# Reordering the seven products of a channel-mixing matmul, with one more PSUM bank, and making the next batch's activations one slot sooner

## The chip, the cores and the metric

The kernel runs on one core of a Trainium2 chip. The metric is the device time of one execution in microseconds (us). A profiled execution also has a span, from its first to its last traced instruction; the device time is 1.8 to 2.1 us longer than the span. In the program, TensorE writes into PSUM tiles (the text calls one of them a bank); the tiles that the other engines make lie in SBUF.

## The reference, cut to what matters

Eight batches of a linear attention feed an MLP mixer. Only the last line matters here.

```python
x = attention(q, k, v)                       # 8 batches x 576 positions x 512
u = x + (relu(x.T @ w_tok1) @ w_tok2).T      # token mixing
out = u + relu(u @ w_ch1) @ w_ch2            # channel mixing, 512 -> 1536 -> 512
```

Inputs and output are float32; the kernel multiplies in bfloat16.

## The kernel before

TensorE is the engine to keep busy. While it does the channel mixing of one batch, the other engines prepare the next batch. The second matmul of the channel mixing, h1 @ w_ch2, is cut into 2 x 2 quadrants and done with seven products instead of eight (in the manner of Strassen and Winograd): fewer matmuls, but sums of quadrants for VectorE, GpSimd and ScalarE. `a11`..`a22` are the quadrants of h1, `quad(i, j)` those of the weights, `t1`, `t2`, `t3`, `t4` sums of these made once, `s1` and `s2` sums of the a's made for every batch, in two parts each. One product is 12 matmuls, 1.31 us. `channel7` does this for six batches and, with `fine=True`, for the tail: the last 64 positions of every batch together, whose 1 MB of output ends the program.

```python
def channel7(uT, u, store, by_slot, hooks, fine=False):
    ...                                       # step(): runs what hangs on the next slot
    for mi in range(NCH):                     # 12 hidden blocks, L667
        c_ps = psM.tile([P, 512], F32, name="c_ps", tag="psM")
        ...
        relu(by_slot[mi], h1[:, mi, :], c_ps)
        if mi == NCH - 2:                     # first part of both sums
            s_part(s1, nc.vector.tensor_add, a21, a22, 0)
            s_part(s2, nc.vector.tensor_sub, s1, a11, 0)
        if mi == NCH - 1:                     # second part of both sums, L652
            s_part(s1, nc.vector.tensor_add, a21, a22, 1)
            s_part(s2, nc.vector.tensor_sub, s1, a11, 1)
        step()
    Dk = bank()                               # then seven products, L657
    ...                                       # fine: A in two halves
    A = bank()
    product(A, a11, quad(0, 0), True)         # first product
    nc.scalar.copy(va, A)
    nc.vector.tensor_sub(a21, a11, a21)
    step()
    product(Dk, a22, t4, True)                # second
    nc.scalar.copy(vb, Dk)
    nc.gpsimd.tensor_sub(u22, u22, vb)
    step()
    Bk = bank()
    product(Bk, s2, t2, True)                 # third: the first reader of s2
    nc.vector.tensor_add(va, Bk, va)
    nc.vector.tensor_sub(s2, a12, s2)
    step()
    C = bank()
    product(C, s1, t1, True)                  # fourth: the first reader of s1
    ...
```

Between two batches the work of the next one (`n`) hangs on these slots. `u_all(i)` is three steps: VectorE adds the token mixing to x (L466), GpSimd casts it to bfloat16 (L265), and the SP queue issues a transposing DMA into `uT` (L473), which the next batch's hidden blocks (L667) read.

```python
at(10, n.u_all, 0)
at(11, n.u_all, 1)                            # slot 11: behind the second part of s1 and s2
...
def store_tail(j, u, n=1, cs=slice(0, Dm)):   # each call: one store on the SP queue, one on ScalarE's
    for c, eng in ((0, nc.sync), (1, nc.scalar)):
        eng.dma_start(out=rows[:, 2 * j + c:2 * (j + n):2, cs], in_=u[c::2, j:j + n, cs])
```

Of the kernel before, what the change touches and what calls it, by code (L numbers as in the profile page):

```python
# [9 lines left out]
F32 = mybir.dt.float32  # L10
# [7 lines left out]
PLAN = """  # L18
feat.0.k.4.2.0.D feat.0.q.0.2.0.A feat.0.q.2.2.1.A feat.0.q.3.2.1.A feat.0.q.4.2.1.D feat.0.q.3.2.0.A
feat.0.q.2.2.0.A mkid ld.1.q.2 warm.0.tr.1.1.43 turn.0.1.1 feat.0.k.3.2.0.A feat.0.k.4.2.1.D turn.0.1.0  # L20
feat.0.q.1.2.1.D feat.0.q.4.2.0.A feat.0.q.1.2.0.A feat.0.k.2.2.0.D feat.0.k.1.2.1.D cast.0.0.3.0.P
warm.0.tr.2.1.7 turn.0.2.1 turno.0.2.1.A feat.0.k.0.2.1.D cast.0.3.2.0.D feat.0.k.1.2.0.D turno.0.1.0.A
feat.0.q.0.2.1.D warm.0.tr.0.0.45 turn.0.0.0 feat.0.k.0.2.0.D turn.0.2.0 turno.0.2.0.D feat.0.k.3.2.1.A
feat.0.k.2.2.1.A cast.0.0.3.1.A turn.0.0.1 wt1 turno.0.1.1.D wt2 cast.0.3.2.1.P kvm.0.1 kvo.0.1.D turno.0.0.1.A
turno.0.0.0.A kvm.0.0 kvo.0.0.A num.0.0.1 numo.0.0.1 feat.1.q.1.2.1.A num.0.2.1 numo.0.2.1 num.0.0.0 numo.0.0.0
# [34 lines left out]
def kernel(  # L60
# [11 lines left out]
    nc = tc.nc  # L72

    B, H, S, D = q.shape
    Dm = H * D
    _, D_tok = moe_w_tok1.shape
    _, D_ch = moe_w_ch1.shape
    P = 128
# [33 lines left out]
    psA = ctx.enter_context(tc.tile_pool(name="psA", bufs=2, space=bass.MemoryType.PSUM))  # L112
# [19 lines left out]
    def heads(g):  # L132
        return slice(0, H) if g == 2 else slice(g * HH, (g + 1) * HH)
# [23 lines left out]
    for n, (t, g) in enumerate(LOADS0):  # L157
        d = load(0, t, heads(g), nc.gpsimd if FIRST == "P" else nc.sync)
# [108 lines left out]
    def relu(eng, dst, src):  # L267
        if eng == "A":
            nc.scalar.activation(dst, src, AF.Relu)  # L269
        else:  # L270
            nc.vector.tensor_relu(dst, src)  # L271
# [342 lines left out]
    K2, D2 = NCH // 2, Dm // 2  # L614
    t2, t3, t4 = (const.tile([P, K2, D2], BF16, name=f"t{i}") for i in (2, 3, 4))

    def quad(a, b):
        return wc2[:, a * K2:(a + 1) * K2, b * D2:(b + 1) * D2]

    t1 = quad(0, 1)  # L620
# [7 lines left out]
    def channel7(uT, u, store, by_slot, hooks, fine=False):  # L628
        h1 = one.tile([P, NCH, 4 * P], BF16, name="h1")
        slot = 0  # L630

        def step():
            nonlocal slot
            for f in hooks.get(slot, ()):
                f()
            slot += 1

        def tok(a, b):
            return h1[:, a * K2:(a + 1) * K2, b * 2 * P:(b + 1) * 2 * P]

        a11, a12, a21, a22 = tok(0, 0), tok(1, 0), tok(0, 1), tok(1, 1)
        s1 = one.tile([P, K2, 2 * P], BF16, name="s1")
        s2 = one.tile([P, K2, 2 * P], BF16, name="s2")
        va = w2r.rearrange("p n s -> p (n s)").bitcast(F32)[:, :2 * D2].rearrange("p (a b) -> p a b", a=2)
        vb = one.tile([P, 2, D2], F32, name="vb")
        vc = one.tile([P, 2, D2], F32, name="vc")
        u11, u12 = u[:, 0:2, :D2], u[:, 0:2, D2:]
        u21, u22 = u[:, 2:4, :D2], u[:, 2:4, D2:]

        def s_part(dst, f, a, b, n):  # L650
            ks = (slice(0, 4), slice(4, K2))[n]
            f(dst[:, ks], a[:, ks], b[:, ks])  # L652

        def product(ps, a, b, first, jjs=(0, 1)):
            for jj in jjs:
                for ki in range(K2):
                    nc.tensor.matmul(ps[jj] if isinstance(ps, list) else ps[:, jj], a[:, ki, jj * P:(jj + 1) * P], b[:, ki],  # L657
                                     start=(first and ki == 0 and (jj == 0 or isinstance(ps, list))), stop=ki == K2 - 1,
                                     skip_group_check=True)

        def bank():
            return psM.tile([P, 2, D2], F32, name="m_ps", tag="psM")

        for mi in range(NCH):
            c_ps = psM.tile([P, 512], F32, name="c_ps", tag="psM")
            for ki in range(NCC):
                nc.tensor.matmul(c_ps, wc1[:, ki, mi * P:(mi + 1) * P], uT[:, :, ki, :],  # L667
                                 start=(ki == 0), stop=(ki == NCC - 1))
            relu(by_slot[mi], h1[:, mi, :], c_ps)
            if mi == NCH - 2:  # L670
                s_part(s1, nc.vector.tensor_add, a21, a22, 0)
                s_part(s2, nc.vector.tensor_sub, s1, a11, 0)
            if mi == NCH - 1:
                s_part(s1, nc.vector.tensor_add, a21, a22, 1)
                s_part(s2, nc.vector.tensor_sub, s1, a11, 1)
            step()
        Dk = bank()
        if fine:
            A = [bank()[:, 0], psA.tile([P, D2], F32, name="m2_ps", tag="psA")]
            for jj in range(2):  # L680
                product(A, a11, quad(0, 0), True, (jj,))
                nc.scalar.copy(va[:, jj], A[jj])
        else:
            A = bank()
            product(A, a11, quad(0, 0), True)
            nc.scalar.copy(va, A)
        nc.vector.tensor_sub(a21, a11, a21)
        step()
        product(Dk, a22, t4, True)
        nc.scalar.copy(vb, Dk)  # L690
        nc.gpsimd.tensor_sub(u22, u22, vb)
        step()
        Bk = bank()
        product(Bk, s2, t2, True)
        nc.vector.tensor_add(va, Bk, va)
        nc.vector.tensor_sub(s2, a12, s2)
        step()
        C = bank()
        product(C, s1, t1, True)
        nc.scalar.copy(vc, C)  # L700
        nc.vector.tensor_add(u12, u12, va)
        nc.gpsimd.tensor_add(u22, u22, vc)
        step()
        product(Dk, a21, t3, False)
        nc.vector.tensor_add(vb, Dk, va)
        step()
        wide = bass.AP(tensor=vb.tensor, offset=vb.offset, ap=[vb.ap[0], [D2, 2], [0, 2], [1, D2]])
        u2 = u[:, 2:4, :].rearrange("p j (a d) -> p j a d", a=2)
        product(C, s2, quad(1, 1), False)
        if fine:  # L710
            nc.vector.tensor_add(u2, u2, wide)
            store(2, u, 2)
            nc.vector.tensor_add(u12, C, u12)
            store(0, u, 2, slice(D2, Dm))
            step()
            for jj in range(2):
                product(A, a12, quad(1, 0), False, (jj,))
                nc.vector.tensor_add(u11[:, jj], A[jj], u11[:, jj])
            store(0, u, 2, slice(0, D2))
        else:  # L720
            nc.vector.tensor_add(u12, C, u12)
            step()
            product(A, a12, quad(1, 0), False)
            nc.vector.tensor_add(u11, A, u11)
            store(0, u, 2)
            nc.vector.tensor_add(u2, u2, wide)
            store(2, u, 2)
        step()
        step()

    def out_rows(b, par, j, n):
# [21 lines left out]
    for word in PLAN.split():  # L753
        name, *a = word.split(".")
        a = [int(x) if x.isdigit() else x for x in a]
# [37 lines left out]
    def hooks7(n, m, nxt, quads):  # L793
        h = {}

        def at(slot, f, *a):
            h.setdefault(slot, []).append(lambda: f(*a))
        if nxt is not None:
            at(0, load, nxt, "k")
            at(0, load, nxt, "q")  # L800
            at(16 if nxt == 5 else 9, load, nxt, "v")
        if n is not None:
            at(0, n.kv_all)
            for j in range(JA):
                at(2 + j, n.num_all, j)
            for j in range(JA):
                at(7 + j // 3, n.mix, j, 2)
            at(8, n.mix_out)
            at(10, n.u_all, 0)
            at(11, n.u_all, 1)  # L810
            at(18, n.u_all, 2)
        if m is not None:
            for j in range(JA):
                at(3 + j, m.cast, j, 1, 2, "P")
            for i, slot in enumerate((1, 2, 3, 4, 5, 6, 9, 10, 11, 12)):
                at(slot, m.feat, "q", i // 2, 2, i % 2, "A")
            for i, slot in enumerate((7, 7, 8, 8, 13, 14, 15, 16, 17, 17)):
                at(slot, m.feat, "k", i // 2, 2, i % 2, "D" if i < 4 else "A")
            at(12, m.turnx, 0, 2)
            at(14, m.turnx, 2, 2)  # L820
            at(15, m.turnx, 4, 1)
        if quads:
            for f, slot in zip(quad_weights(), (0, 0, 0, 8)):
                at(slot, f)
        return h
# [4 lines left out]
    for p in range(2, B):  # L830
        s = bt[p]
        n = bt[p + 1] if p + 1 < B else None
# [8 lines left out]
    _ = tile, bass_utils  # L841
# [30 lines left out]
```

## Time and profile before

| | before |
|---|---|
| time, median of 4 runs | 270.46 us (270.08 to 271.02) |
| span of the profiled execution | 267.7 us |
| TensorE busy | 254.9 us (95%) |
| first of the seven products starts, first `channel7` batch | 104.8 us |
| TensorE ends | 261.7 us |
| last store lands | 266.0 us |

The lines themselves are in the prediction. The table is read as three stretches: up to 105 us nothing in question happens; from there to TensorE's end lie six batches and the tail; after TensorE's end come the last sums and stores. The second and third stretches are what the change can touch.

### The profile page before, as it was taken

What the parts mean: (1) busy time and instruction counts of PE and PEld (TensorE: products, weight loads), DVE (VectorE), ACT (ScalarE), POOL (GpSimd) and SP (SyncE); (2) the same over time, 40 slices, a digit from 0 to 9 for tenths busy, and PEclk for the clock granted to TensorE, in tenths of its full rate; (3) what the DMA queues carried; (4) which work ended last, traced back from release to release, by engine and by line L of the source; (5) the groups of instructions that cost most, each with busy time, mean ns of one, the idle gap of its engine ahead of it and who ended that gap; (6) DMA issues with size and microseconds to landing.
All of it is one profiled execution on the core that took longest, in us unless ns stands there. A gap on an engine that the chain in (4) does not pass through costs nothing.

```text
span 267.7 us, 5480 instructions
## 1 busy us (share of the span) xinstructions
PE 254.9 (95%) x2165; PEld 161.5 (60%) x2181; DVE 202.3 (76%) x367; ACT 143.8 (54%) x236; POOL 76.7 (29%) x82
## 2 busy tenths in 40 slices
PE   6998999999999999999998999999999999999991
PEld 2785556456444555855585558645865585585580
DVE  6489798799892879969895869686958596564572
ACT  2796272473591576829782788378753423323410
POOL 2173070040033261702475007420710072030030
PEclk9999999999999999999999999999999999999997
DMA  6999999999999999999999995950393044003004
GB/s 201 361 255 165 243 258 229 365 224 214 343 287 181 288 374 369 128 182 326 288 326 183 306 366 131 178 196 2 74 204 156 0 81 162 14 2 157 0 2 158
DMA packets 79146, 53.41 MB, mean 200 GB/s; under 512 B 47761, under 2 KB 76689, under 8 KB 79121
## 3 DMA queue, kind: packets, MB, share of 16 engines
q1 hardware_dynamic: 74544, 48.77, 68.8%
q0 software_dynamic: 4144, 3.77, 9.3%
q10 hardware_dynamic: 432, 0.52, 0.5%
q8 instruction: 17, 0.28, 0.4%
q14 instruction: 9, 0.07, 0.1%
HBM read 35.85 MB, written 9.44 MB: 169 GB/s over the span
## 4 chain that ended last, share of the span: by engine, by line
PE 67%; DMA 12%; issue 5%; POOL 4%; DVE 4%; SPq 4%; ACT 1%; DVEq 0%; POOLq 0%; ACTq 0%
PE c_ps L667 20%; PE m_ps L657 16%; PE c L513 5%; PE b L434 5%; PE o L525 4%; DMA uT<-ub 4%; PE kv L362 3%; PE u L461 3%; POOL ub L265 3%; DMA qpT<-qp 3%; DMA vt<-in_v_dram 3%; DMA kt<-in_k_dram 3%; PE wm L193 3%; PE tr L312 2%; SPq L144 2%
## 5 line engine op out<-in xcount | busy, mean ns | idle before, releaser
L667 PE MATMUL c_ps<-uT,wc 128*128 128x512 bf16 x288 | 70.4, 379 | 2.0 <-DMA uT<-ub 1.0
L269 ACT ACTIVATE h<-c_ps 128x512 bf16<-128x512 f32 x66 | 39.3, 596 | 49.6 <-PE c_ps L667 32.0
L667 PEld LDWEIGHTS <-wc 128*128 128x128 bf16 x336 | 30.8, 97 | 34.5 <-issue 1.8
L265 POOL CAST ub<-u 128x1024 bf16<-128x1024 f32 x14 | 19.0, 1357 | 78.7 <-DVE u L466 72.5
L657 PEld LDWEIGHTS <-h 128*128 128x128 bf16 x336 | 32.9, 98 | 5.3
L331 ACT ACTIVATE qp<-qt,cos_t 128x512 bf16<-128x512 f32 x33 | 23.4, 720 | 21.0 <-DMA qt<-in_q_dram 11.5
L265 POOL CAST vbf<-vt 128x512 bf16<-128x512 f32 (+3 forms) x28 | 18.7, 703 | 39.9 <-DMA vt<-in_v_dram 38.3
L271 DVE TENSOR_SCALAR h<-c_ps 128x512 bf16<-128x512 f32 x18 | 12.4, 688 | 20.0 <-PE c_ps L667 20.0
L657 PEld LDWEIGHTS <-s 128*128 128x128 bf16 x252 | 24.7, 98 | 2.8
L513 PE MATMUL c<-uT,wc 128*128 128x512 bf16 x96 | 22.7, 379 | 0.1
L525 PE MATMUL o<-wc,h 128*128 128x512 bf16 x92 | 21.6, 379 | 0.2
L414 DVE TENSOR_TENSOR x<-nf,den 128x512 bf16<-128x512 f32 x30 | 20.7, 691 | 1.0
L331 ACT ACTIVATE qp<-qt,sin_t 128x512 bf16<-128x512 f32 x30 | 21.4, 722 | 0.0
L391 PEld LDWEIGHTS <-qpT 128*128 128x128 bf16 x320 | 15.2, 98 | 10.1 <-DVE x L414 1.5
L657 PE MATMUL m_ps<-wc,h 128*128 128x256 bf16 x168 | 20.6, 273 | 0.0
L657 PE MATMUL m_ps<-t,h 128*128 128x256 bf16 x168 | 20.6, 273 | 0.0
L657 PE MATMUL m_ps<-wc,s 128*128 128x256 bf16 x168 | 20.6, 273 | 0.0
L466 DVE TENSOR_TENSOR u<-u,x 128x1024 f32<-128x1024 f32 x16 | 19.3, 1215 | 1.0 <-PE u L461 1.0
L434 PE MATMUL b<-x,w 128*128 128x512 bf16 (+1 forms) x84 | 19.8, 353 | 0.3
L331 ACT ACTIVATE kp<-kt,sin_t 128x512 bf16<-128x512 f32 x21 | 14.8, 715 | 3.3 <-DMA kt<-in_k_dram 3.3
L461 PE MATMUL u<-B,w 128*128 128x512 bf16 x64 | 16.1, 379 | 0.0
L331 ACT ACTIVATE kp<-kt,cos_t 128x512 bf16<-128x512 f32 x22 | 15.4, 719 | 0.3 <-DMA kt<-in_k_dram 0.3
(117 smaller groups left out, 388.9 us busy)
## 6 DMA issues: line engine op xcount, KB each, us to landing
out_dram<-u SPq DMA_DIRECT2D x32, 256.0 KB, 4.0
qt<-in_q_dram SPq DMA_DIRECT2D x8, 640.0 KB, 7.4
kt<-in_k_dram SPq DMA_DIRECT2D x8, 640.0 KB, 8.0
qt<-in_q_dram SPq DMA_DIRECT2D x8, 512.0 KB, 5.9
kt<-in_k_dram SPq DMA_DIRECT2D x8, 512.0 KB, 6.8
vt<-in_v_dram SPq DMA_DIRECT2D x6, 640.0 KB, 8.9
vt<-in_v_dram SPq DMA_DIRECT2D x6, 512.0 KB, 7.6
wc<-in_moe_w_ch_dram POOLq DMA_DIRECT2D x4, 384.0 KB, 7.9
```

The lines of the kernel that those rows point to most:

```text
L265: (nc.scalar.copy if eng == "A" else ENG[eng].tensor_copy)(dst, src)
L269: nc.scalar.activation(dst, src, AF.Relu)
L331: nc.scalar.activation(dst, src, AF.Relu, scale=tab)
L391: nc.tensor.matmul(nm[:, hh * (D + 1):(hh + 1) * (D + 1)], self.qpT[:, j * H + h, :], self.kv[:, h, :D + 1], start=(not eps or hh == 0), s ...
L414: nc.vector.tensor_mul(dst, nmv[:, :, :, :D], den_b)
L434: nc.tensor.matmul(b1[:, mi], w1[:, col(self.c, j), mi * P:(mi + 1) * P], self.x[:, j, cs], start=(j == 0 and (g == 2 or mi == 0)), stop=( ...
L461: nc.tensor.matmul(ps[:, jj], w2[:, ki, 1 + 2 * g + jj, :], self.B1[:, ki, :], start=(ki == 0), stop=(ki == NT - 1))
L466: nc.vector.tensor_add(self.sb("u")[:, js, :], self.ps.pop(("u", g)), self.x[:, js, :])
L513: nc.tensor.matmul(ps, wc1[:, ki, mi * P:(mi + 1) * P], self.uT[:, :, ki, :], start=(ki == 0), stop=(ki == NCC - 1))
L525: nc.tensor.matmul(self.ps["o", j], self.h1[:, ki, j * P:(j + 1) * P], wc2[:, ki, :], start=(ki == 0), stop=(ki == NCH - 1))
L657: nc.tensor.matmul(ps[jj] if isinstance(ps, list) else ps[:, jj], a[:, ki, jj * P:(jj + 1) * P], b[:, ki], start=(first and ki == 0 and (j ...
L667: nc.tensor.matmul(c_ps, wc1[:, ki, mi * P:(mi + 1) * P], uT[:, :, ki, :], start=(ki == 0), stop=(ki == NCC - 1))
```

## The change

Its intent: the next batch's u is made before the last hidden block's sums instead of after them, so that its transpose lands before TensorE asks for it. The products come in another order. The fourth product gets a PSUM bank of its own (five banks instead of four), so that `u21` takes it straight from PSUM and one ScalarE copy goes. The tail gets an order of its own, so that its stores can be spread over its last products.

```diff
-        Dk = bank()
-        ...                                   # A, Dk, B(s2), C(s1), Dk+=, C+=(s2), A+=
+        def p1():                             # A = a11 q00; va = A
+        def p2():                             # A += a12 q10; u11 += A; fine: store
+        def p3():
+            product(ps["C"], s1, quad(1, 1), False)
+            nc.vector.tensor_add(u12, ps["C"], u12)
+            store(0, u, 2, slice(D2, Dm) if fine else slice(0, Dm))
+        def p4():
+            ...                               # fine: two halves, then the last store
+                E = bank()                    # the fifth bank
+                product(E, a22, t4, True)
+                nc.vector.tensor_add(u21, E, u21)
+        def p5():
+            ps["C"] = bank()
+            product(ps["C"], s1, t1, True)
+            nc.scalar.copy(vc, ps["C"])
+            nc.vector.tensor_sub(s1, a12, s2)
+            nc.gpsimd.tensor_add(u22, u22, vc)
+        def p6():                             # B = s2 t2; va += B; u12 += va
+        def p7():
+            ps["D"] = bank()
+            product(ps["D"], a21, t3, True)
+            nc.vector.tensor_add(vb, ps["D"], va)
+            nc.gpsimd.tensor_add(u21, u21, vb)
+            nc.vector.tensor_add(u22, u22, vb)
+            store(2, u, 2, slice(D2, Dm) if fine else slice(0, Dm))
+        def s3():                             # a21 = a11 - a21
+        order = (p1, s3, p5, p6, p7, p3, p2, p4) if fine else (p1, s3, p4, p2, p5, p6, p7, p3)
@@
-            at(11, n.u_all, 1)
+            at(10, n.u_all, 1)
@@
-            for i, slot in enumerate((1, 2, 3, 4, 5, 6, 9, 10, 11, 12)):
+            for i, slot in enumerate((1, 2, 3, 4, 5, 7, 9, 10, 11, 12)):
```

More of the change, by code (lines that the diff above doesn't have):

```diff
@@ L676, in channel7 @@
             step()
-        Dk = bank()
-        if fine:
-            A = [bank()[:, 0], psA.tile([P, D2], F32, name="m2_ps", tag="psA")]
-            for jj in range(2):
-                product(A, a11, quad(0, 0), True, (jj,))
-                nc.scalar.copy(va[:, jj], A[jj])
-        else:
-            A = bank()
-            product(A, a11, quad(0, 0), True)
-            nc.scalar.copy(va, A)
-        nc.vector.tensor_sub(a21, a11, a21)
-        step()
-        product(Dk, a22, t4, True)
-        nc.scalar.copy(vb, Dk)
@@ L691, in channel7 @@
-        nc.gpsimd.tensor_sub(u22, u22, vb)
-        step()
-        Bk = bank()
-        product(Bk, s2, t2, True)
-        nc.vector.tensor_add(va, Bk, va)
-        nc.vector.tensor_sub(s2, a12, s2)
-        step()
-        C = bank()
-        product(C, s1, t1, True)
-        nc.scalar.copy(vc, C)
-        nc.vector.tensor_add(u12, u12, va)
-        nc.gpsimd.tensor_add(u22, u22, vc)
-        step()
-        product(Dk, a21, t3, False)
-        nc.vector.tensor_add(vb, Dk, va)
-        step()
@@ L707, in channel7 @@
-        wide = bass.AP(tensor=vb.tensor, offset=vb.offset, ap=[vb.ap[0], [D2, 2], [0, 2], [1, D2]])
-        u2 = u[:, 2:4, :].rearrange("p j (a d) -> p j a d", a=2)
-        product(C, s2, quad(1, 1), False)
-        if fine:
-            nc.vector.tensor_add(u2, u2, wide)
-            store(2, u, 2)
-            nc.vector.tensor_add(u12, C, u12)
-            store(0, u, 2, slice(D2, Dm))
-            step()
-            for jj in range(2):
-                product(A, a12, quad(1, 0), False, (jj,))
-                nc.vector.tensor_add(u11[:, jj], A[jj], u11[:, jj])
-            store(0, u, 2, slice(0, D2))
-        else:
-            nc.vector.tensor_add(u12, C, u12)
-            step()
-            product(A, a12, quad(1, 0), False)
-            nc.vector.tensor_add(u11, A, u11)
-            store(0, u, 2)
-            nc.vector.tensor_add(u2, u2, wide)
-            store(2, u, 2)
@@ L728, in channel7 @@
-        step()
+        ps = {}
+        def p1():
+            ps["A"] = bank()
+            product(ps["A"], a11, quad(0, 0), True)
+            nc.scalar.copy(va, ps["A"])
+        def p2():
+            product(ps["A"], a12, quad(1, 0), False)
+            nc.vector.tensor_add(u11, ps["A"], u11)
+            if fine:
+                store(0, u, 2, slice(0, D2))
+        def p3():
+            product(ps["C"], s1, quad(1, 1), False)
+            nc.vector.tensor_add(u12, ps["C"], u12)
+            store(0, u, 2, slice(D2, Dm) if fine else slice(0, Dm))
@@ new lines, in p4 @@
+        def p4():
+            if fine:
+                E = [psA.tile([P, D2], F32, name="m2_ps", tag="psA") for _ in range(2)]
+                for jj in range(2):
+                    product(E, a22, t4, True, (jj,))
+                    nc.vector.tensor_add(u21[:, jj], E[jj], u21[:, jj])
+                store(2, u, 2, slice(0, D2))
+            else:
+                E = bank()
[7 more added lines that the diff above has]
+            nc.gpsimd.tensor_add(u22, u22, vc)
@@ new lines, in p6 @@
+        def p6():
+            ps["B"] = bank()
+            product(ps["B"], s2, t2, True)
+            nc.vector.tensor_add(va, ps["B"], va)
+            nc.vector.tensor_add(u12, u12, va)
+        def p7():
[5 more added lines that the diff above has]
+            store(2, u, 2, slice(D2, Dm) if fine else slice(0, Dm))
@@ L729, in channel7 @@
+        def s3():
+            nc.vector.tensor_sub(a21, a11, a21)
+        order = (p1, s3, p5, p6, p7, p3, p2, p4) if fine else (p1, s3, p4, p2, p5, p6, p7, p3)
+        for f in order:
+            f()
+            if f is not s3:
+                step()
         step()
```

## The prediction

> **What bounds the kernel now.** I read the page's busy table first, then TensorE's own waits (who it waited for, and how long), then the timeline around the places where it waited, then the chain of work at the end.
>
> ```profile
> span 267.7 us, 5480 instructions
> PE 254.9 (95%) x2165; PEld 161.5 (60%) x2181; DVE 202.3 (76%) x367; ACT 143.8 (54%) x236; POOL 76.7 (29%) x82
> ```
>
> TensorE is busy for 254.9 us of a span of 267.7, so 12.8 us is all that any change which leaves the matmuls alone could win. This change leaves them alone: the built order has 4364 rows on TensorE before and after. The question is which of the 12.8 us it touches. The waits of TensorE in the stretch where the changed code runs (100 to 262 us) are few:
>
> ```profile
> PE c_ps L667 <- DMA uT<-ub: 1.0, 2, 0.6
> PE c_ps L667 <- ACT h L269: 0.9, 2, 0.5
> PE nf L391 <- DMA qpT<-qp: 0.2, 1, 0.2
> ```
>
> The reader is to see three releasers and 2.1 us in total, each wait under 0.6 us. The rest of the idle time is at the start (2.3 us for a first operand, before anything that is changed) and at the end: TensorE ends at 261.7, so 6.0 us of the span lie after it. The timeline of the second boundary between batches shows how one of these waits arises:
>
> ```profile
> 132.57 1.17 POOL L265 CAST ub<-u 128x1024 bf16<-128x1024 f32 x1 [3.36 <-DVE u L466]
> 132.88 1.14 DVE L652 TENSOR_TENSOR s<-s,h 128x512 bf16<-128x512 bf16 x1
> 133.94 1.21 DVE L466 TENSOR_TENSOR u<-u,x 128x1024 f32<-128x1024 f32 x1
> 135.22 1.70 POOL L265 CAST ub<-u 128x1024 bf16<-128x1024 f32 x1 [1.47 <-DVE u L466]
> ...
> 141.75 1.02 PE L667 MATMUL c_ps<-uT,wc 128*128 128x512 bf16 x4 [0.45 <-DMA uT<-ub]
> ```
>
> Columns are start, duration, engine, line, operation. The second half of u for the next batch is added at 133.94, behind two sums for the seven products; its cast ends at 136.92, its transposing DMA is issued at 136.94 and lands at 141.61 (the chain of waits gives "DMA uT<-ub" 4.67 us), and the next batch's first matmul stands still for it. The end of the program reads:
>
> ```profile
> 259.22 0.69 DVE L705 TENSOR_TENSOR vb<-m_ps,w2r 128x512 f32<-128x512 f32 x1 [0.46 <-PE m_ps L657]
> 260.01 1.23 DVE L711 TENSOR_TENSOR u_tail<-u_tail,vb 128x1024 f32<-128x1024 f32 x1
> 261.16 0.68 DVE L713 TENSOR_TENSOR u_tail<-m_ps,u_tail 128x512 f32<-128x512 f32 x1
> 261.27 2.16 SPq L747 DMA_DIRECT2D out_dram<-u_tail  x3
> 261.27 2.31 ACTq L747 DMA_DIRECT2D out_dram<-u_tail  x3
> 261.76 0.74 DVE L718 TENSOR_TENSOR u_tail<-m_ps,u_tail 128x256 f32<-128x256 f32 x2
> ```
>
> All 1 MB of tail output is issued after 261.27, the first half in the largest stores, so the last store is issued behind two others on each queue (ending at 263.43 and 263.59) and lands at 265.64 and 266.01.
>
> **What the Trainium skill says.** "Perfetto Trace Analysis", Optimization Strategy, says to take the most-contended engine, find the gaps between its slices and the semaphore that ends each; the waits above are that list. "GPSIMD Engine Reference", Specifications, says that GpSimd's SBUF interfaces are shared with VectorE, with contention when the VectorE instruction has two SBUF inputs. The trace agrees: the add of two f32 SBUF tiles (L701) takes 0.68 us in the tail with GpSimd idle at its start and 1.75 us in the batches where GpSimd is at an add of its own, and at 132.88 a sum that takes 0.42 us elsewhere takes 1.14 beside a cast. In these overlaps the one that started first keeps its speed and the other mostly stands. "DMA: Bandwidth & Descriptors", Anatomy of one DMA, puts the fixed part of a DMA at about 2.0 us, mostly the receipt of the last byte; the first tail store lands 1.91 us after its issue ends, the last 2.2 and 2.4, so 0.3 to 0.5 us is queueing behind the earlier data. The same page (Issuing engines are not separate DMA queues) says that two issuing engines save issue time only, so I expect nothing from where the four stores stand, only from when.
>
> **The change part by part.**
>
> (a) u a slot sooner. The two u products now precede the last hidden block, and the second u add follows the first on VectorE. It moves from 133.94 to about 132.5; its cast then runs straight after the first cast, ends near 135.0 to 135.4 instead of 136.92, and the DMA can be issued about 1.5 us sooner (at the first boundary 108.5 instead of 110.05; at the third 162.7 instead of 164.61). The qpT transposes behind it on the same issuing queue move by as much, and so does all that ScalarE waits for there: at 175.93 its qp feature starts after 3.12 us of waiting for a qpT transpose, the relu behind it is late, and TensorE waits 0.54 us. The five waits are 0.56 and 0.45 (uT), 0.22 (qpT), 0.32 and 0.54 (ScalarE): 2.09 us. 1.5 us more room is over twice the largest. But between 131 and 148 us the DMA engines' share is at or above 1.0, and there an earlier issue is not wholly an earlier landing. I take 85%: **-1.8 us**.
>
> (b) The order of the products. 84 matmuls of a 0.109 us pitch (12 in 1.31 us) per batch, as before: 0. It lets u21 take its product straight from PSUM, so one ScalarE copy (0.585 us x7 = 4.1 us) goes, on an engine that is 54% busy and here waits for TensorE: 0 on the path. VectorE gets two adds of 0.69 us (u21 from PSUM, u22 plus vb) for the wide one of 1.22 to 1.27: nothing on the path.
>
> (c) The fifth bank. The built program's waits show that the first four blocks of the next batch take their banks in the order of release, so that the last product's bank is taken by the fourth block only, 2.6 us or more after the product ends. The late adds on VectorE (below) therefore should not hold TensorE. The second product into the first bank now comes 1.31 us after the first one ends, and must wait for ScalarE's copy out of it; that copy ends 0.78 us after (133.06 to 133.84): 0.5 us of margin.
>
> (d) The tail. The last product is now the one in two halves into u21, so VectorE has only 0.41 us left after the last half, and three of four stores are issued before. But u21 plus vb on GpSimd (1.27 us) starts 0.06 us after vb and u22 plus vb on VectorE 0.10 us after it, as handoffs of these two kinds take elsewhere; so by the rule above VectorE stands until GpSimd is done: vb ends at 258.6, u22 near 260.5, then 0.68 + 0.68 + 0.41 + 0.41 with small overlaps gives 262.6 against 262.50 before. The last issue ends near 263.4, lands after about 1.95 us instead of 2.2 to 2.4, near 265.4: 0.6 us sooner. If VectorE gets in first, 262.25 and 1.0 us. I take **-0.6 us**. Against it: the second product of the tail now reads s1, whose second half is ready at 254.09 when its fifth weight load is due at 254.04; with the semaphore some **+0.1 us**.
>
> (e) A q feature from slot 6 to 7: ScalarE's order is the same after the build, as slot 7's relu is on VectorE. 0.
>
> Sum: -1.8 - 0.6 + 0.1 = -2.3 us; 270.67 - 2.3 = 268.4. I add 0.2 for small waits that I have not seen: **268.6 us**, 0.8% faster.
>
> **The rivals.**
>
> R1: VectorE becomes what TensorE waits for. At each boundary u22 plus vb beside GpSimd's u21 plus vb would stretch from 0.69 to some 1.8 us, and u12, which frees the last bank, comes after. For the last batch I get u12 done at 244.5 in the clock of before, and the fourth block is due at 244.6: it just fits. If the second block needed that bank it would be due at 242.9, and the wait 1.6 us there and 1.2 at the boundary before. For R1: VectorE is 76% busy, and the margin is 0.1 us. Against: the built waits name u12 at the fourth block. It would make the time 269 to 271.
>
> R2: the DMA engines are the bound at the boundaries, so earlier issues land no sooner. For it: the share of 1.07 from 130 to 138 us. Against: at the third boundary the share from 164 to 166 us is 0.08, the queue waits for work. It would leave about 0.9 of the 2.1 us: 269.3.
>
> R3: the copy out of the first bank comes late behind a ScalarE feature (0.72 us each), and TensorE waits 0.2 us in each of four batches: 269.4.
>
> **Range and chances.** All of (a) and the good tail give 267.4; R1 with R2 gives about 270.6. 8 in 10: 267.3 to 270.3. Two per cent is 5.4 us, more than twice all the waits that the change can reach, so faster by that has 0.02; for slower by it some new wait of over 1 us per batch is needed, for which I find no place: 0.01.
>
> **What would show each step.** (a) The uT and both ScalarE waits are gone from TensorE's list, and the second uT transpose is issued 1.3 us or more closer to the first. (b) TensorE's busy time is 254 to 256 us, ScalarE's 4 us less. (c) No wait of c_ps for VectorE's u L692; if it stands there, R1 is right. (d) The last store's landing lies 3.7 us (before 4.3) after TensorE's last matmul, and u22 plus vb (L725) lasts some 1.8 us. The prediction is wrong if a new releaser with over 1 us stands in TensorE's waits, or if the span falls by more than 3 us.

(One clause is cut: for stores that SP and ScalarE issue, it took a figure from a section that is about DMAs issued by GpSimd. Step (d) does not need it; it works with the 1.91 us of the trace. "The same page" is "DMA: Bandwidth & Descriptors". The 4364 rows are of the author's build; the traces have 2165 matmuls and 2181 weight loads, before and after.)

## The result, and the profile after

The changed kernel takes **266.81 us** (median of 4 runs, 266.27 to 267.53) against 270.46 before: ratio 0.9865 [0.9834, 0.9896]. Ratios here are the mean time of one kernel's runs over that of the other's of the same rounds, so not quite the ratio of the medians; a change "by ratio" is the ratio's distance from 1 times 270. The gain is 3.65 us, where 2.1 were predicted, and the time lies 0.5 us below the predicted range. Later the same kernel gave 0.9880 [0.9857, 0.9903], a gain of 3.2 us. I take 3.2 as the size to explain: it is also the difference of the two profiled executions (269.8 and 266.64). The two intervals overlap, so the other 0.4 can be scatter.

The head and the busy table of the page after:

```profile
span 264.9 us, 5478 instructions
...
PE 254.6 (96%) x2165; PEld 161.6 (61%) x2181; DVE 203.9 (77%) x374; ACT 139.6 (53%) x228; POOL 69.2 (26%) x82
```

TensorE does the same work in the same time, and ScalarE does 4.2 us less. TensorE's waits in the stretch of the batches (who was waited for: us in total, times, longest) are down from 2.1 us to one line:

```profile
PE c_ps L667 <- ACT h L269: 0.2, 1, 0.2
```

Why, shows the timeline of the second boundary (start, duration, engine, line, operation; x2 is two of them in one line):

```profile
130.80 2.35 DVE L466 TENSOR_TENSOR u<-u,x 128x1024 f32<-128x1024 f32 x2
...
132.09 2.30 POOL L265 CAST ub<-u 128x1024 bf16<-128x1024 f32 x2 [4.41 <-DVE u L466]
...
133.52 1.14 DVE L652 TENSOR_TENSOR s<-s,h 128x512 bf16<-128x512 bf16 x1
...
140.86 1.03 PE L667 MATMUL c_ps<-uT,wc 128*128 128x512 bf16 x4
```

Both u adds run back to back, both casts follow without the 1.47 us gap of before, and the second part of `s2` (133.52, which before stood between the two adds) now comes last. The next batch's first matmul at 140.86 carries no bracket: it waits for nothing.

The end of the program, where before all stores were issued after 261.27 with TensorE ending at 261.7; here TensorE ends at 259.69:

```profile
256.66 1.26 POOL L724 TENSOR_TENSOR u_tail<-u_tail,vb 128x512 f32<-128x512 f32 x1 [1.29 <-DVE vb L723]
256.68 1.79 DVE L725 TENSOR_TENSOR u_tail<-u_tail,vb 128x512 f32<-128x512 f32 x1
...
258.39 0.68 DVE L692 TENSOR_TENSOR u_tail<-m_ps,u_tail 128x512 f32<-128x512 f32 x1
258.50 2.76 SPq L754 DMA_DIRECT2D out_dram<-u_tail  x4
258.50 3.02 ACTq L754 DMA_DIRECT2D out_dram<-u_tail  x4
258.99 0.68 DVE L686 TENSOR_TENSOR u_tail<-m_ps,u_tail 128x512 f32<-128x512 f32 x1
259.59 0.74 DVE L700 TENSOR_TENSOR u_tail<-m_ps,u_tail 128x256 f32<-128x256 f32 x2
```

The first stores go 1.2 us before TensorE's end instead of 0.46. They would go sooner still, but `u22 + vb` on VectorE lasts 1.79 us for 0.68 us of work: GpSimd's `u21 + vb` started 0.02 us ahead of it, and VectorE stands until that is done. So the stores that waited for it are bunched behind 258.50.

By stretches, in the profiled executions; the second pair is the same two kernels, profiled again later (the controls below):

| us | before | after | change | second pair | change |
|---|---|---|---|---|---|
| start of the first product | 104.84 | 104.86 | 0.0 | 106.37, 105.48 | -0.89 |
| from there to TensorE's end | 156.89 | 154.83 | -2.06 | 155.87, 154.68 | -1.18 |
| TensorE's end to the last landing | 4.27 | 3.66 | -0.61 | 4.28, 3.66 | -0.61 |
| last landing to the end of the span | 1.66 | 1.51 | -0.16 | 1.66, 1.50 | -0.16 |
| device time less span | 2.13 | 1.78 | -0.35 | 2.13, 1.78 | -0.35 |

The last three rows together, unrounded, are 8.07 us before and 6.94 after, in both pairs. All five are -3.2 in both pairs too, but not for the same reason: the first two rows scatter from execution to execution, by a microsecond and more over all profiles. So the tail's share is known to about a tenth, and that of the batches only as a mean of several profiles.

### The profile page after: what moved, and what is told of

It reads as the page before. It is cut to its first block, busy times and chain, and to the rows that moved or that the text cites. A ratio compares the mean times of both kernels' runs of the same rounds, so it can differ in the third digit from the quotient of the medians.

```text
span 264.9 us, 5478 instructions
## 1 busy us (share of the span) xinstructions
PE 254.6 (96%) x2165; PEld 161.6 (61%) x2181; DVE 203.9 (77%) x374; ACT 139.6 (53%) x228; POOL 69.2 (26%) x82
## 4 chain that ended last, share of the span: by engine, by line
PE 93%; DVE 2%; DMA 1%; issue 1%; ACT 1%; DVEq 0%; ACTq 0%
PE c_ps L667 26%; PE m_ps L657 24%; PE c L513 8%; PE o L525 8%; PE b L434 6%; PE u L461 5%; PE kv L362 4%; PE wm L193 3%; PE nf L391 3%; PE tr L312 2%; PE tr L346 2%; PE ut L489 1%; DMA qpT<-qp 1%; PE nm L391 1%; DVE x L414 1%
## 5 line engine op out<-in xcount | busy, mean ns | idle before, releaser
L265 POOL CAST ub<-u 128x1024 bf16<-128x1024 f32 x14 | 15.5, 1112 | 69.0 <-DVE u L466 62.5
L712 POOL TENSOR_TENSOR u<-u,vc 128x512 f32<-128x512 f32 x6 | 8.5, 1416 | 27.7 <-ACT vc L710 27.7
```

Source lines behind the costliest of these rows:

```text
L265: (nc.scalar.copy if eng == "A" else ENG[eng].tensor_copy)(dst, src)
```

## The experiments

The theory to test (T): the gain has two independent parts, waits at the boundaries removed by the sooner u, and a tail whose stores are spread; the order of the products in the batches is worth nothing by itself. A first rival: the order itself brings the larger than predicted gain. A second: the sooner u alone brings what the boundaries gain, and neither order nor fifth bank is needed. Each call had its own runs of the kernel before (medians 269.85, 270.23 and 270.26 us, 11 runs each); every experiment had 4 to 6 runs, and all gave the right result.

### The parts alone

**Only u sooner**, in the kernel before:

```diff
-            at(11, n.u_all, 1)
+            at(10, n.u_all, 1)
```

> The kernel before with one change: the second u product of the next batch a slot sooner; products, tail and stores as before. Theory (the five waits of TensorE at the boundaries, 0.56+0.45+0.22+0.32+0.54 = 2.09 us, all come from a late second uT transpose and the qpT transposes queued behind it): 2.0 to 2.1 us faster than before, no uT and at most one short ScalarE wait left in TensorE's list; TensorE's last matmul at 259.7 instead of 261.7, and the 6.0 us after it unchanged. Rival (the order of the products carries part of it, by freeing banks or VectorE sooner): 1 us or less.

Measured: 269.38 us, ratio 0.9981 [0.9959, 1.0003]: a gain of 0.5 us, perhaps none, and not two. The old waits for uT, qpT and ScalarE are gone from the list of TensorE's waits, as in the changed kernel, but a new one stands in their place:

```profile
PE m_ps L657 <- DVE s L652: 1.2, 5, 0.2
```

The timeline of the third boundary shows it:

```profile
157.70 2.35 DVE L466 TENSOR_TENSOR u<-u,x 128x1024 f32<-128x1024 f32 x2
...
160.42 1.14 DVE L652 TENSOR_TENSOR s<-s,h 128x512 bf16<-128x512 bf16 x1
...
160.78 0.60 PE L657 MATMUL m_ps<-t,s 128*128 128x256 bf16 x4
...
161.61 1.05 PE L657 MATMUL m_ps<-t,s 128*128 128x256 bf16 x8 [0.23 <-DVE s L652]
```

The two u adds now stand before the second part of `s2`, which becomes ready at 161.56; the third product, its reader, started at 160.78, did the four matmuls that need only the first part, and stopped. The bracket says 0.23 us, but the block of seven products takes 9.74 us instead of 9.33 in five batches: 0.41 each, 2.05 us in all, about what the removed waits had given: the stretch from the first product to TensorE's end takes 156.45 us, where six profiles with u in its old slot have 156.4 in the mean. So T is wrong in its word "independent", and the second rival is wrong too.

**All but the sooner u**, the changed kernel with `at(11, n.u_all, 1)`:

> The changed kernel with the second u product put back to its old slot: new order of products everywhere, new tail, four stores. Theory: only the tail gains, 0.7 to 0.8 us faster than before, and the waits for uT, qpT and ScalarE are back with some 2.1 us. Rival (the order shares in the gain at the boundaries): 1.5 us or more faster.

Measured: 269.02 us, ratio 0.9960 [0.9937, 0.9983], a gain of 1.1 us by ratio. Boundary waits are back, but only 0.8 us of them in this profile (for ScalarE and qpT), where 2.1 were expected. Going from here to the whole change gains 0.9960 - 0.9880, that is 2.2 us (each against its own runs of before; some 0.9 us either way): the same one-line edit that was worth 0.5 in the old order.

**Only the tail's order and stores**, batches and slot as before (`channel7` has both bodies, the new one under `if fine:`):

> The kernel before with the new order and the four stores in the tail alone. Theory: 0.7 to 0.8 us faster than before, all of it after TensorE's last matmul (5.2 us instead of 6.0). Rival: the new tail needs the order of the earlier batches (banks released otherwise), 0.4 us or less.

Measured: 268.67 us, ratio 0.9962 [0.9937, 0.9986], a gain of 1.0 us. After TensorE's end come 7.07 us of device time instead of 8.07, and the last store lands 3.67 us after it instead of 4.27.

**Only the order in the batches**, with the old tail (the new body under `if not fine:`), and once more:

> The kernel before with the new order of products in the batches alone, old tail, old slot of u. Theory: 0 (within 0.3 us); ScalarE's busy time 3.5 us less, TensorE's waits as before. Rival R1 of the prediction (VectorE late with its adds holds TensorE): slower by 0.5 us or more; rival of order sharing in the gain: faster by 0.5 us or more.

> e4_mid_only once more (its times were 0.6 us above before, its profile 0.2 below in span). Theory (the order alone is worth 0 at the boundaries): within 0.4 us of before, and TensorE's waits at the boundaries as before (1.0 to 2.1 us). Rival (VectorE's later adds cost something that the profiled execution did not show): again 0.5 us or more slower, with a wait of c_ps for VectorE or longer waits for DMAs in the profile.

Measured: 270.86 us, ratio 1.0022 [0.9994, 1.0050], and 270.00 us, ratio 0.9989 [0.9966, 1.0012]. By ratio +0.6 and -0.3: nothing that can be told from 0. The second execution's waits are those of before:

```profile
PE c_ps L668 <- DMA uT<-ub: 1.0, 2, 0.5
PE c_ps L668 <- ACT h L270: 0.6, 2, 0.4
PE nf L392 <- DMA qpT<-qp: 0.2, 1, 0.2
```

(The lines are one higher because this copy has a comment line more.) So the order removes no wait by itself, and the first rival falls: the order is worth 0 without the sooner u, and about 1.7 us with it (3.2, less 1.0 of the tail and 0.5 of the sooner u).

### What in the order makes the sooner u pay

The order changes several things at once. The question is whether TensorE needs only that `s2` be read later, or the fifth bank and the dropped copy as well. I took the sooner u and the old order, and exchanged only the third and fourth products, so that `s1` is read third and `s2` fourth.

```diff
-        product(Bk, s2, t2, True)      # third
-        nc.vector.tensor_add(va, Bk, va)
-        nc.vector.tensor_sub(s2, a12, s2)
-        product(C, s1, t1, True)       # fourth
-        nc.scalar.copy(vc, C)
-        nc.vector.tensor_add(u12, u12, va)
+        product(C, s1, t1, True)       # third
+        nc.scalar.copy(vc, C)
+        product(Bk, s2, t2, True)      # fourth
+        nc.vector.tensor_add(va, Bk, va)
+        nc.vector.tensor_sub(s2, a12, s2)
+        nc.vector.tensor_add(u12, u12, va)
```

> The kernel before with u a slot sooner and ONE swap in the old order: the product that reads s1 third, the product that reads s2 fourth. Four banks, all copies, the old tail. Theory (u sooner pays only if no product needs s2 in the third place: run e1_u_only lost 5 x 0.41 us = 2.05 us waiting for the late s2): the waits of m_ps for the s sums are gone, 2.0 to 2.6 us faster than before (ratio 0.990 to 0.993). Rival (the fifth bank or the dropped ScalarE copy is what makes room): about 0.5 us faster like e1_u_only.

Measured: 274.34 us, ratio 1.0157 [1.0137, 1.0176]. A miss, and a badly built test. The old wait is gone, but there is a larger one:

```profile
PE m_ps L657 <- DVE s L701: 5.4, 7, 0.9
```

`s2` is written again, as a12 - s2, for the sixth product. I had moved that with its first reader, to behind the fourth product:

```profile
166.32 1.44 DVE L701 TENSOR_TENSOR s<-h,s 128x1536 bf16<-128x1536 bf16 x1
...
167.82 1.48 PE L657 MATMUL m_ps<-wc,s 128*128 128x256 bf16 x12 [0.91 <-DVE s L701]
```

It cannot start before the add of the fourth product is done, and lasts until 167.76; the product that reads it was due at 166.75. The changed kernel avoids this by writing the same sum into `s1`, which is free once the product that reads s1 is done. So the next run does that and nothing else: 

```diff
         nc.scalar.copy(vc, C)
+        nc.vector.tensor_sub(s1, a12, s2)      # right behind the third product
...
-        nc.vector.tensor_sub(s2, a12, s2)
...
-        product(C, s2, quad(1, 1), False)
+        product(C, s1, quad(1, 1), False)
```

> Run e7_u_swap done right: u sooner, s1 product third, s2 product fourth, and a12 minus s2 written into s1 as soon as the third product has read it (in e7 it went into s2, which was free only after the fourth product, 1.3 us before its use: TensorE waited 0.9 us in each of seven batches). Still four banks, all three ScalarE copies, old tail. Theory (the gain of u sooner needs only that s2 is read later and s1 rewritten early): TensorE's waits for sums are gone, and it is 2.0 to 2.6 us faster than before (span 265.3 to 265.9). Rival (fifth bank or dropped copy needed): 1 us or less.

Measured: 267.52 us, ratio 0.9904 [0.9876, 0.9932], a gain of 2.6 us with four banks, three ScalarE copies and the old tail. No wait of TensorE is left in the batches. The same boundary as above:

```profile
157.57 2.35 DVE L466 TENSOR_TENSOR u<-u,x 128x1024 f32<-128x1024 f32 x2
...
160.28 1.14 DVE L652 TENSOR_TENSOR s<-s,h 128x512 bf16<-128x512 bf16 x1
...
160.65 1.47 PE L657 MATMUL m_ps<-wc,s 128*128 128x256 bf16 x12
...
161.96 1.47 PE L657 MATMUL m_ps<-t,s 128*128 128x256 bf16 x12
```

`s2` is as late as in the first experiment (161.42), but TensorE does another product first, and the reader of `s2` starts at 161.96 with 0.5 us in hand, its 12 matmuls in one piece. So what the sooner u needs of the order is that `s2` be read one product later, and its rewriting early enough. The fifth bank and the dropped copy were not needed for this gain.

### The tail

**u21 + vb of the tail on VectorE**, in the changed kernel, behind `u12`, so that nothing on GpSimd stands in the way of `u22 + vb`; the same kernel again:

```diff
 # p7
-            nc.gpsimd.tensor_add(u21, u21, vb)
+            if not fine:
+                nc.gpsimd.tensor_add(u21, u21, vb)
 # end of p3
+            if fine:
+                nc.vector.tensor_add(u21, u21, vb)
```

> The changed kernel with one edit in the tail: u21 plus vb goes from GpSimd to VectorE, after u12. Theory (in the changed tail u22 plus vb took 1.79 us beside GpSimd instead of 0.68, which held all four stores to one bunch from 258.50 to 261.52): u22 plus vb 0.68 us, first store issued 1.1 us sooner, last store landing 0.5 to 0.7 us sooner, time 0.5 to 0.7 us less than the changed kernel. Rival (the last store is bound by the last product alone): 0.2 us or less.

> e5_tail_dve once more, beside e9_best: ratio 0.984 to 0.988 to before; first-store-to-last-landing and the time after TensorE's last matmul (4.5 us) as in e5_tail_dve.

Measured: 266.28 us, ratio 0.9856 [0.9833, 0.9879], and 265.79 us, ratio 0.9842 [0.9817, 0.9867]. The end:

```profile
257.42 0.69 DVE L728 TENSOR_TENSOR u_tail<-u_tail,vb 128x512 f32<-128x512 f32 x1
...
258.03 0.68 DVE L692 TENSOR_TENSOR u_tail<-m_ps,u_tail 128x512 f32<-128x512 f32 x1
258.14 3.38 SPq L757 DMA_DIRECT2D out_dram<-u_tail  x4
258.15 3.42 ACTq L757 DMA_DIRECT2D out_dram<-u_tail  x4
...
260.47 0.42 DVE L702 TENSOR_TENSOR u_tail<-m_ps,u_tail 128x256 f32<-128x256 f32 x1 [0.22 <-PE m_ps L657]
```

`u22 + vb` takes 0.69 us where it stood for 1.79. VectorE has one add more, yet it waits for TensorE at the very end (the bracket) instead of running behind it. The first store goes 2.29 us before TensorE's end, and the last lands 3.00 us after it instead of 3.66. Device time after TensorE's end is 6.31 us against 6.94.

What sets the last landing shows when the tails are laid side by side. From the first store's issue to the last landing pass 4.74 to 4.76 us in all seven profiles with the old tail, and 4.85 or 4.86 in the four with the changed one. The stores have the DMA engines busy meanwhile (share 1.01 from 263 to 264 us before, 1.02 from 260 to 262 after). So the changed tail lands sooner because its first store is issued 1.19 us instead of 0.46 before TensorE's end; that the last issue ends 1.83 us after TensorE's end, against 1.86, cannot be it. The three profiles with a new order in the batches and the old tail agree: their first store goes only 0.09 to 0.13 us ahead, and the last landing comes 4.62 to 4.65 us after TensorE's end. With the VectorE tail 5.30 us pass: there the last store, issued 0.5 us after TensorE's end, lands 2.5 us later, and the share falls to 0.77, so the last product and no longer the first store seems to be the bound.

**Controls**, the changed kernel and the kernel before, unchanged:

> The changed kernel again, beside the others of this call: ratio 0.985 to 0.989 to before if the first measurement holds on this chip. Theory: sum of the order alone with its tail (e2_order_all, 0.8 to 1.1 us) and of u sooner on top of it (2.5 us).

> The kernel before once more, for a second profile and the spread: ratio 1.000 within 0.003. Theory for the 0.8 us that the times moved more than the profiles did: TensorE's waits for DMAs at the boundaries vary from run to run, and the first profile had a low draw; this profile would show 2.1 to 3 us of such waits. Rival: the same 2.1 us within 0.2, and the difference is noise of the times.

Measured: 267.02 us, ratio 0.9880 [0.9857, 0.9903], and 270.10 us, ratio 0.9996 [0.9977, 1.0016]. Against the first, the VectorE tail gains 0.74 us in the medians, and 0.64 us in the traces. The profile of the second shows how far the list of waits varies from one execution to the next:

```profile
PE c_ps L668 <- DMA uT<-ub: 0.5, 1, 0.5
PE c_ps L668 <- ACT h L270: 0.4, 1, 0.4
```

That is 0.9 us, where the first profile of the same kernel had 2.1. The expectation is missed: the first profile's list was not a low draw but the longest. In the six profiles with u in its old slot the lists add up to 0.8 to 2.1 us.

### The best version

The VectorE tail, and the q features of the next batch moved a slot later, since the one boundary wait left after the change was for a relu on ScalarE behind such features:

```diff
-            for i, slot in enumerate((1, 2, 3, 4, 5, 7, 9, 10, 11, 12)):
+            for i, slot in enumerate((2, 3, 4, 5, 6, 7, 9, 10, 11, 12)):
```

> The kernel of e5_tail_dve with the first six q features of each batch a slot later, so that the relu of the third block no longer stands behind a feature that waits for the qpT transpose. Theory (the last boundary wait, 0.40 us in the fourth batch, is that relu): 0.2 to 0.4 us faster than e11_tail_dve_again, no c_ps wait left. Rival: the features only move the wait to a later relu: the same within 0.2.

Measured: 265.90 us (265.78 to 266.23), ratio 0.9837 [0.9812, 0.9863]. In its trace the first four distances from one batch's first product to the next one's are all 26.40 us (after the change one was 26.80), so the last wait is gone. But against the run of the VectorE tail alone (mean 265.95 against 266.09) the difference is within the scatter. Both versions beat the changed kernel.

The runs together, by ratio to the kernel before:

| kernel | gain, us |
|---|---|
| sooner u alone | 0.5 |
| order in the batches alone | -0.6, 0.3 |
| tail alone | 1.0 |
| order and tail, u as before | 1.1 |
| sooner u, two products exchanged, sum into s2, old tail (the miss) | -4.2 |
| sooner u, two products exchanged, sum into s1, old tail | 2.6 |
| the whole change | 3.65, 3.2 |
| the same, tail's u21 + vb on VectorE | 3.9, 4.3 |
| the same, q features a slot later | 4.4 |

## Why the prediction was right or wrong

The time was below the range. The step that failed is the size of (d): its mechanism is right, but the tail was put at -0.6 us and measured -1.13. A second error, taking (b) as independent of (a), left the total alone, because the change does both. The batches, (a), came out near the forecast: 1.65 us in the mean of the traces against a net 1.5. Together that is 2.8 us of the kernel's own, where 2.1 were predicted. The other 0.4 to 0.9 us of the two measured gains (3.2 and 3.65) is not found in the stretches that were changed: in the second pair 0.89 us lies before the first product, where the kernels are all but alike.

- **(a) u a slot sooner, "I take 85%: -1.8".** The mechanism is as predicted: the uT and qpT waits are gone, and the second uT transpose of the third boundary is issued 1.34 us after the first instead of 3.18. Of the two ScalarE waits one of 0.2 us is left, and in the second profile none. The size is right as far as the traces can tell. From the first product to TensorE's end pass 155.75 to 157.01 us in the six profiles with u in its old slot (before, twice; order alone, twice; tail alone; both: mean 156.42), and 154.68 to 154.83 in the four with the changed batches (the change, twice; VectorE tail, twice: mean 154.77): 1.65 us, where the working has -1.8 + 0.1 + 0.2 = -1.5. The first pair alone (2.06) would have the discount too large, the second (1.18) too small. To come so near was partly luck: the second profile of the same kernel has 0.9 us of waits to remove, and 85% of that is 0.8. The saturated DMA engines (R2) cost no more than the 0.4 us of the one boundary that is 26.80 instead of 26.40 us long. The stall foreseen for the tail's second product was at most 0.05 us.
- **(b) "0".** Right for the order alone, in two runs. Wrong in adding it to (a) as an independent term. In the old order the sooner u pushes the second part of `s2` behind the u adds and gives back five times 0.41 us at the third product. I had the line for it in front of me: in the boundary that the prediction quotes, that sum ends at 134.02, and its reader starts at 134.37 and needs it from its fifth matmul on, 4 x 0.109 us later, at 134.81. So there were 0.79 us of room, and 1.21 us of u add to come in ahead: 0.42 us short, and 0.41 was measured. The total survived this because the change does both.
- **(c) The fifth bank, and R1.** Right: no wait for `u12` (L692) appears, and the copy out of the first bank held up nothing, so R3 falls too. It did not need to be there, as the four-bank run shows.
- **(d) The tail, "-0.6".** Its mechanism came out to the tenth: GpSimd's add started 0.02 us ahead, `u22 + vb` lasted 1.79 us (predicted 1.8), and the last store landed 3.66 us after TensorE's end (predicted 3.7). The term is mis-sized all the same, and this is the step that failed: it prices the landing only, and by the device time the new tail is worth 8.07 - 6.94 = 1.13 us, in both pairs, and 1.0 in the run of the tail alone. 0.16 us of the rest lies in the span behind the landing, 0.35 outside it, where no trace reaches. Even this split is open. The kernels with a new order in the batches and the old tail have the span 6.30 us beyond TensorE's end instead of 5.94, and only 1.77 or 1.78 us outside it, like the changed kernel; their device time after TensorE's end is 8.08 to 8.10 all the same. Measured against them, the whole 1.13 us is in the span, and 0.98 of it in the landing (4.64 to 3.66). What sets the part outside the span was not found.
- **(e) "0".** Right: copies left out, ScalarE has the same 207 instructions in the same order in the traces with slot 6 (before, the exchange into s1) and with slot 7 (after).
- **Range and chances.** The within-2% class was right. The lower end, 267.3, stood on "all of (a) and the good tail", 267.4; these terms give 267.6 (270.67 - 2.1 - 1.0). It had no room for a tail worth more than its landing, nor for the scatter of four runs (the ratio's interval is 0.8 us either way). One profile's list of waits was too thin a ground for a sum told to a tenth.

The condition named for being wrong, a span falling by more than 3 us, did not occur in the profiles (267.7 to 264.9, 2.8 us); the device time fell by more than the span.

## What to carry to other kernels

When work is moved ahead on an engine, look for who else is in that queue: the item pushed back is due to a reader, and the room that this reader has is in the timeline already. A reorder that gains nothing by itself can be what makes another edit pay, so test such parts together as well as alone. At the end of a program, issue the first store as early as you can, keep GpSimd's adds of two SBUF tiles out of the way of VectorE's last chain, and measure the gain by the device time, not by the landing.

## What the Trainium skill lacked or had wrong

- "GPSIMD Engine Reference", Specifications, says only that there is contention on the shared SBUF interfaces; who wins and for how long is not there. In these runs it is exclusive: GpSimd's add of two f32 tiles kept its 1.26 us, and VectorE's, begun 0.02 us later, took 1.79 us instead of 0.69; with GpSimd idle it took 0.69. "SBUF — State Buffer", SBUF: two separate sides, does say this ("exclusive lock, not a bandwidth split"), and these runs agree with it; so the skill as a whole does not lack it.
- "DMA: Bandwidth & Descriptors", Issuing engines are not separate DMA queues, calls the issue time "usually small relative to the DMA itself". For the tail's 128 KB stores it was not small: four of them took the SP queue 2.76 us to issue (0.69 each), against a median of 2.2 us from issue to landing. What that costs is not shown: the DMA engines were busy at the same time (share 1.02).
- No page tells that equal stores land later from ScalarE's queue than from SP's: a median of 2.5 us against 2.2 from issue to landing, after the change and with the VectorE tail alike. ScalarE's store of each pair was never issued first (it came up to 0.25 us later), so whether the queue or the order does it is not separated.
- No page tells why the device time outside the traced span should differ from kernel to kernel. It was 2.13 or 2.14 us in four profiles (before, twice; the sooner u alone; the first exchange), 1.91 with the changed tail alone, and 1.77 to 1.81 in the other nine. Its cause stays open.
